# Spectrum in pairs, a shorter way from the last pieces to the first token blocks, and the last gate at the activation, in a state-space and token-mixing kernel on one core

## The chip, the cores and the metric

The kernel runs on one core of a Trainium2 chip. The metric is the device time of one execution in microseconds (us), given as the median of several runs. The core has five engines with an instruction stream each: TensorE (PE; its weight loads stand as PEld), VectorE (DVE), ScalarE (ACT), GpSimd (POOL) and SyncE (SP), which here issues DMA transfers. Engines wait for each other by semaphores.

## The reference

The input x has 2048 tokens of 448 channels, all float32. A vector c gives six modulation vectors; the block applies a long convolution with a kernel made from a state-space model (through an FFT of length 4096), then a two-layer network across tokens:

```python
x = A_u
mod = (_silu(c) @ w_mod).reshape(c.shape[0], 6, 1, -1)
sa, ca, ga, sb, cb, gb = (mod[:, 0], mod[:, 1], ...)
h = _layernorm(x) * (1 + ca) + sa
x = x + ga * _A_ref(h, ...)      # y = irfft(rfft(h) * rfft(K)) + h * D_skip
h = _layernorm(x) * (1 + cb) + sb
x = x + gb * _B_ref(h, ...)
# _B_ref: h = layernorm(x); u = gelu(w1^T over tokens + b1), 1792 wide;
#         y = w2^T over those + b2, 2048 tokens
```

## The kernel before

The work runs in five stages.

**The kernel and the spectrum** (to about 348 us of the span). TensorE makes the convolution kernel from the state-space parameters and the spectrum of h. The spectrum lies in DRAM as `us_d`, split into two halves of the channels ("chunks", 224 channels each, `DC`).

**The pieces.** Each chunk has 16 pieces (`NP`) of two frequencies. Piece n asks for its part of the spectrum (`u`) and its table (`si`) in `pc_load`; ACT makes a copy with the two halves of the partitions exchanged (`pc_swap`, tile `sw`), POOL completes the table with three operations (`pc_tables`), TensorE makes the convolution kernel's spectrum (`pc_s2`, tile `kx`), DVE multiplies (`pc_mul`, tiles `z0`, `z1`), TensorE transforms a first step back (`pc_inv`, tile `vv`), and ACT copies the result to SBUF (tile `vt` of `pc_out`), from where it is written to `v_d` in DRAM. The first chunk's pieces 0 to 15 are spread over the stage before. The second chunk's, 16 to 31, are the loop near the end of the listing: at step k the load of piece n+3, `kx` and the products of piece n, the table and the exchanged copy of piece n+1, and the way back of piece n−1.

**The head of the network.** The 2048 tokens are 16 blocks r of 128. `ln_load` reads a block's rows back from `v_d` (again tiles called `vt`), `ln_y` makes the last transform step with the table `ft` into PSUM (`y`) and adds it to x, and `stats`, `ln_mod` and `ln_out` make the two layer norms in a row, whose result is kept as a high and a low part (`h3h`, `h3l`). Until the first blocks are ready `warm` issues multiplies whose result nothing reads.

**The first layer**, `mlp1`: 14 tiles of 128 hidden units, in two halves of seven accumulators `acc`, each over the 16 blocks, with three matmuls for each pair (high by high, high by low, low by high). `gelu` empties the seven accumulators through ACT into `u`, of which three buffers exist, and DVE splits it into `uh` and `ul`. Both parts of a half are made in that order, f = 0 to 6, and the next half begins in the same order.

**The second layer**: 16 token tiles, each 42 matmuls into `o`, then bias, gate and residual on DVE and the write to the output.

Three more things set the order. PE, ACT, DVE and POOL run in the order of the code. SP does so too where a `manual_schedule` of SP is open (from step k = 12 of the second chunk on); before that a scheduler places its transfers. SP's queue is in order: a transfer whose data isn't ready holds up those behind it, and each waits for the one eight before it. The weights come through `wst`: `load` asks for one, `ahead` (or `begin` and `rest`) splits one into `whi` on ACT and `wlo` on DVE.

Of the kernel before, what the change touches and what calls it, by code (L numbers as in the profile page):

```python
# [15 lines left out]
ALU = mybir.AluOpType  # L16
# [21 lines left out]
WAHEAD = 4  # L38


def dft_tables():
# [66 lines left out]
    order = lambda a: a.reshape(P, 32, 2, 2, 2, 16).swapaxes(3, 4)  # L108
# [11 lines left out]
    t["FT"] = ft.reshape(P, 64)  # L120

# [99 lines left out]
def tile_adaln_s4d_mixer(ctx, tc, i, out):  # L221
# [20 lines left out]
    with ExitStack() as es:  # L242
# [520 lines left out]
        pl, pz, pv, pk = {}, {}, {}, {}  # L763
# [4 lines left out]
        def pc_load(n):  # L768
            c, p = divmod(n, NP)
            u = fp.tile([P, 2, 2, DC], F32, tag="u", name="u", bufs=3)  # L770
            if c:
                nc.sync.dma_start(u[:, 0], us_d[c, :, 2 * p : 2 * p + 2])
# [3 lines left out]
            w = fp.tile([P, 3, 2, P], F32, tag="si", name="si", bufs=4)  # L776
# [4 lines left out]
            pl[n] = u, w  # L781
# [3 lines left out]
        def pc_swap(n):  # L785

            pw[n] = swp.tile([P, 2, DC], F32, tag="sw", name="sw")
            for h in range(2):
                S.copy(pw[n][64 * h : 64 * h + 64], pl[n][0][64 - 64 * h : 128 - 64 * h, 0])

        def pc_tables(n):


            like, unlike = pl[n][1][:, 1], pl[n][1][:, 2]
            G.tensor_copy(unlike[0:64], like[64:128])
            G.tensor_copy(unlike[64:128], like[64:128])
            G.tensor_scalar(like[64:128], like[0:64], -1.0, None, ALU.mult)

        def pc_s2(n):
            c, p = divmod(n, NP)  # L800
            k1 = yks[c][:, 2 * p : 2 * p + 2]
            pk[n] = (pxs if c else pms).tile([P, 2, DC], F32, tag="ms", name="kx")
            for j in range(2):
                T.matmul(pk[n][:, j], pl[n][1][:, 0, j], k1[:, j], start=True, stop=True)  # L804

        def pc_mul(n):
            c, p = divmod(n, NP)
            u = pl[n][0]
            pz[n] = []
            for cc in range(2):  # L810
                z = fp.tile([P, 2, DC], F32, tag=f"z{cc}", name=f"z{cc}")
                V.tensor_tensor(z, pk[n], pw.pop(n) if c and cc else u[:, cc], ALU.mult)  # L812
                pz[n].append(z)
            pk.pop(n)

        def pc_inv(n):
            pv[n] = pms.tile([P, 2, DC], F32, tag="ms", name="vv")
            w, z = pl.pop(n)[1], pz.pop(n)
# [4 lines left out]
        def pc_out(n, copy=S.copy):  # L823
            c, p = divmod(n, NP)
            vt = swp.tile([P, 2, DC], F32, tag="vt", name="vt", bufs=4) if c else fp.tile([P, 2, DC], F32, tag="vt", name="vt")
            copy(vt, pv.pop(n))
            rows = v_d[2 * p : 2 * p + 2, :, c * DC : (c + 1) * DC]
# [342 lines left out]
        swp = es.enter_context(tc.tile_pool(name="swp", bufs=2))  # L1170
        pc_swap(NP)
# [27 lines left out]
        for n in range(2):  # L1199
            wst.ahead(n + 1, nc.vector, False)  # L1200


    with ExitStack() as es:
# [9 lines left out]
        v_v = v_d.rearrange("k (ch g r) d -> r (k ch) g d", ch=4, g=2)  # L1213
# [12 lines left out]
        vts, hs, sa, sb = {}, {}, {}, {}  # L1226

        def ln_load(r):
            vts[r] = rot.tile([P, 2, D], F32, tag="vt", name="vt", bufs=4)
            nc.sync.dma_start(vts[r], v_v[r])  # L1230
# [6 lines left out]
        def stats(src, total, tag):  # L1237

            mean, ss, rs = (small(nm, tag) for nm in ("mean", "ss", "rs"))
            V.tensor_scalar(mean, total, -1.0 / D, None, ALU.mult)  # L1240
            sq = rot.tile([P, D], F32, tag="sq", name="sq")
            S.activation(sq, src, AF.Square, bias=mean, accum_out=ss)
            S.activation(rs, ss, AF.Sqrt, scale=1.0 / D, bias=eps_t)
            return mean, rs

        def ln_y(r):
            y = py.tile([P, D], F32, tag="y", name="y")
            vt = vts.pop(r)
            for g in range(2):
                nc.tensor.matmul(y[64 * g : 64 * g + 64], ft, vt[:, g], start=True, stop=True)  # L1250
# [33 lines left out]
        for r in range(4):  # L1284
            ln_load(r)
            if r == 1:
                x_pair(2)
# [8 lines left out]
        for t in range(-3, 16):  # L1296
            if t < 0:
                warm((9, 1, 2)[t + 3])
# [33 lines left out]
        def gelu(acc, fh):  # L1332
            for f in range(7):
                k = 7 * fh + f
                u = ru.tile([P, D], F32, tag="u", name="u")
                S.activation(u, acc[f], AF.Gelu_apprx_tanh, bias=b1[:, k : k + 1])
                V.tensor_copy(uh[fh][:, f], u)
                V.tensor_tensor(ul[fh][:, f], u, uh[fh][:, f].bitcast(F32), ALU.subtract)
# [14 lines left out]
        for t in range(16):  # L1353
# [14 lines left out]
            V.scalar_tensor_tensor(y, o, b2[:, t : t + 1], mod[5], ALU.add, ALU.mult)  # L1368
            V.tensor_tensor(y, y, xt, ALU.add)
# [28 lines left out]
```

## Time and profile before

| | |
|---|---|
| median of three runs | 698.44 us (696.92 to 700.45) |
| the profiled execution | 699.5 us |
| its span | 697.7 us, mean granted clock 0.988 |
| TensorE busy | 646.5 us |
| second chunk, first `kx` to last `vv` | 354.81 to 393.53 us |
| first matmul of `mlp1` | 408.49 us |
| first activation of `gelu`, first half | 488.08 us |
| last matmul's first follower on DVE | 693.28 us |

The rows that follow are from one profiled execution. A timeline row has the start, the duration, the engine, the line of the code, the operation, out<-in, partitions and elements, how many instructions it stands for, and in brackets the idle time before it with what ended it. TensorE's records overlap, since matmuls are pipelined: the distance from one start to the next is the cost of one. "SPq" is SP issuing a transfer, "DMA" the transfer itself.

### The profile page before, as it was taken

The page shows a single profiled execution, that of the slowest core. Times are in us where ns is not written, and L with a number is a line of the kernel's source. Part 1 is how long each engine was busy: PE and PEld are TensorE (multiplying, and loading weights), DVE is VectorE, ACT ScalarE, POOL GpSimd, SP SyncE. Part 2 cuts the span into 40 slices and gives each one's busy share as a digit, 9 for nine tenths or more (in the row PEclk, how much of TensorE's full clock was granted, in tenths as well). Part 3 has the DMA queues.
Part 4 walks back from the last instruction along what each step waited for, and adds up shares of the span by engine and source line. Part 5 has one row for each costly group of instructions (what it writes and reads, how often), then busy time and mean ns, then how long its engine had stood idle before and what let it go on. Part 6 is the DMA issues. An engine that isn't in the chain of part 4 may idle for free.

```text
span 697.7 us, 18532 instructions
## 1 busy us (share of the span) xinstructions
PE 646.5 (93%) x7314; PEld 486.1 (70%) x7314; DVE 424.1 (61%) x811; ACT 448.5 (64%) x841; POOL 274.7 (39%) x364
## 2 busy tenths in 40 slices
PE   0868999999988899999999989999999999999997
PEld 0444454455545676676789747778999999999996
DVE  7877889787575584857744368777622354444431
ACT  5787698899879899999766568877422332222220
POOL 6694669588588767777546200000000000000000
PEclk9998999999999999999999999999999999999999
DMA  7595647588785486554579899974683445555640
GB/s 183 178 194 143 214 163 241 212 234 268 213 266 165 126 170 170 145 157 120 142 235 301 257 278 244 236 177 135 174 247 108 146 132 159 159 158 165 169 129 28
DMA packets 101894, 128.04 MB, mean 184 GB/s; under 512 B 13547, under 2 KB 85231, under 8 KB 101807
## 3 DMA queue, kind: packets, MB, share of 16 engines
q1 hardware_dynamic: 100606, 123.31, 63.0%
q0 software_dynamic: 1200, 3.54, 2.4%
q8 instruction: 58, 0.95, 0.6%
q14 instruction: 30, 0.24, 0.1%
HBM read 91.46 MB, written 34.87 MB: 181 GB/s over the span
## 4 chain that ended last, share of the span: by engine, by line
PE 68%; ACT 10%; DMA 8%; DVE 6%; issue 4%; POOL 3%; SPq 1%; DVEq 0%; ACTq 0%; POOLq 0%
PE xe L621 7%; PE acc L1222 7%; PE o L1365 6%; PE o L1364 6%; PE o L1366 6%; PE acc L1223 6%; PE acc L1224 6%; PE kg L711 6%; DMA si<-in_SK_dram 3%; PE xg L621 3%; PE pu L542 2%; PE pu L574 2%; PE vv L820 2%; PE kx L804 2%; PE vv L821 2%
## 5 line engine op out<-in xcount | busy, mean ns | idle before, releaser
L206 ACT CAST whi<-w 128x896 fp32r<-128x896 f32 x64 | 59.8, 938 | 134.9 <-PE o L1365 84.6
L215 DVE TENSOR_TENSOR wlo<-w,whi 128x896 fp32r<-128x896 f32 x64 | 68.1, 1088 | 43.1 <-ACT whi L206 36.8
L684 POOL TENSOR_TENSOR G<-mag,gs 128x512 f32<-128x512 f32 x56 | 71.9, 1283 | 50.9 <-ACT gs L680 47.1
L1222 PE MATMUL acc<-h3h,whi 128*128 128x448 f32 x224 | 82.7, 369 | 0.8 <-ACT h3h L1273 0.8
L1223 PE MATMUL acc<-h3l,whi 128*128 128x448 f32 x224 | 81.5, 364 | 0.7 <-DVE h3l L1280 0.5
L1365 PE MATMUL o<-ul,whi 128*128 128x448 f32 x224 | 81.3, 363 | 0.0
L1364 PE MATMUL o<-uh,whi 128*128 128x448 f32 x224 | 81.2, 362 | 0.0
L1224 PE MATMUL acc<-h3h,wlo 128*128 128x448 f32 x224 | 80.7, 360 | 0.0
L1366 PE MATMUL o<-uh,wlo 128*128 128x448 f32 x224 | 80.6, 360 | 0.0
L711 PEld LDWEIGHTS kg<-E,G 128*32 128x32 f32 x3584 | 56.6, 114 | 32.3 <-issue 22.2
L711 PE MATMUL kg<-E,G 128*32 128x64 f32 x3584 | 66.4, 228 | 6.7 <-issue 6.1
L685 POOL TENSOR_TENSOR G<-mag,gs 128x512 f32<-128x512 f32 x56 | 71.8, 1282 | 0.0
L621 PE MATMUL xg<-tab,lph 64*128 64x512 f32 x112 | 62.3, 556 | 5.1 <-ACT gs L680 2.4
L621 PE MATMUL xe<-tab,lph 64*128 64x512 f32 x112 | 62.2, 555 | 1.1 <-ACT gs L681 0.9
L686 DVE TENSOR_TENSOR E<-m,xe 128x512 f32<-128x512 f32 x53 | 36.4, 687 | 41.3 <-ACT xe L679 24.3
L1368 DVE SCALAR_TENSOR_TENSOR y<-o,b,mod 128x448 f32<-128x448 f32 x16 | 10.9, 684 | 80.2 <-PE o L1366 80.2
L665 POOL TENSOR_TENSOR m<-mag,w 128x512 f32<-128x512 f32 x53 | 56.0, 1056 | 4.3 <-DMA u<-us_d 0.2
L1222 PEld LDWEIGHTS acc<-h3h,whi 128*128 128x128 f32 x224 | 42.0, 188 | 13.9 <-ACT h L1278 5.6
L812 DVE TENSOR_TENSOR z<-kx,u 128x448 f32<-128x448 f32 x48 | 28.4, 620 | 27.7 <-PE kx L804 27.7
L1223 PEld LDWEIGHTS acc<-h3l,whi 128*128 128x128 f32 x224 | 42.1, 188 | 3.3 <-DVE h3l L1280 0.8
L1364 PEld LDWEIGHTS o<-uh,whi 128*128 128x128 f32 x224 | 42.0, 188 | 3.4
L621 PE MATMUL xe<-tab,lex 64*128 64x512 f32 x56 | 28.9, 531 | 16.6 <-DMA lex<-wm 15.8
(233 smaller groups left out, 1512.1 us busy)
## 6 DMA issues: line engine op xcount, KB each, us to landing
w<-in_B_w_dram SPq DMA_DIRECT2D x64, 224.0 KB
w<-in_B_w_dram SPq DMA_DIRECT2D x32, 448.0 KB
u<-us_d SPq DMA_DIRECT2D x48, 224.0 KB
yu_d<-yt SPq DMA_DIRECT2D x16, 448.0 KB
yi<-yu_d SPq DMA_DIRECT2D x32, 224.0 KB
us_d<-uo SPq DMA_DIRECT2D x16, 448.0 KB
v_d<-vt SPq DMA_DIRECT2D x32, 224.0 KB
vt<-v_d SPq DMA_DIRECT2D x16, 448.0 KB
```

Source lines behind the costliest of these rows:

```text
L206: self.nc.scalar.copy(hi, w)
L215: eng.tensor_tensor(lo, w, hi.bitcast(F32), ALU.subtract)
L621: T.matmul(out[k], lhs[r], rhs[r], start=start, stop=stop)
L684: G.tensor_tensor(Gt[:, 1], mg_, v32(sg), ALU.mult)
L685: G.tensor_tensor(Gt[:, 0], mg_, v32(cg_), ALU.mult)
L711: T.matmul(kg[32 * q : 32 * q + 32, m], Gt[:, c, d], E[:, c, d], start=h == 0 and c == 0 and m == 0, stop=h == 1 and c == 1, skip_group_ch ...
L1222: nc.tensor.matmul(acc[f], hi[:, fs], h3h[:, r], start=r == 0, stop=False)
L1223: nc.tensor.matmul(acc[f], hi[:, fs], h3l[:, r], start=False, stop=False)
L1224: nc.tensor.matmul(acc[f], lo[:, fs], h3h[:, r], start=False, stop=r == 15)
L1364: nc.tensor.matmul(o, hi[:, ks], uh[kh][:, k], start=kh == 0 and k == 0, stop=False)
L1365: nc.tensor.matmul(o, hi[:, ks], ul[kh][:, k], start=False, stop=False)
L1366: nc.tensor.matmul(o, lo[:, ks], uh[kh][:, k], start=False, stop=kh == 1 and k == 6)
```

## The change

1. The second chunk's spectrum is read for two pieces in one transfer (128 rows of 896 numbers instead of twice 448), four pieces ahead. Its tables have two more buffers, in another pool, and are asked for five pieces ahead instead of three. SP's transfers run in the order of the code from the end of step k = 0.
2. The rows of `v_d` are laid out in another order, by which a block's read has one run of both halves (`g`) for a row. Blocks 0 and 1 are read in two parts: the first chunk's columns at k = 2 and 4, the second chunk's columns of the first 26 rows at k = 14 (`v_half`). The last three pieces (`LAST`) go to these two blocks out of SBUF, by six matmuls for a block with the new table `fl`, which POOL clears with three memsets of 32 x 1536 and a transfer of 192 KB fills.
3. The first weight and the first pair of x are asked for at k = 11, the second weight at k = 12, and the first weight is split before the last copy of a piece.
4. `stats` takes the square with the sum as bias and D as scale, so that ACT doesn't wait for DVE's mean.
5. `warm` has 1, 1 and 3 multiplies instead of 9, 1 and 2.
6. The last gate `mod[5]` is multiplied to `u` behind the activation, not at the output: 14 more DVE operations of 128 x 448. In the second half the cast to `uh` goes to ACT. At the output `mod[5] * b2 + xt` is made before the matmuls end, and one addition stays behind them.

The diff, cut:

```diff
-            u = fp.tile([P, 2, 2, DC], F32, tag="u", name="u", bufs=3)
             if c:
-                nc.sync.dma_start(u[:, 0], us_d[c, :, 2 * p : 2 * p + 2])
+                nc.sync.dma_start(u.rearrange("p n k d -> p (n k d)"), us_d[c, :, 2 * p : 2 * p + 4].rearrange("p k d -> p (k d)"))
+                pu[n], pu[n + 1] = u[:, 0:1], u[:, 1:2]
...
+        def pc_w(n, pool=None):
+            c, p = divmod(n, NP)
+            w = (pool or fp).tile([P, 3, 2, P], F32, tag="si", name="si", bufs=2 if pool else 4)
...
+            if n >= 2 * NP - LAST:
+                vlast.append(vt)
...
+        v_v = v_d.rearrange("k (r ch g) d -> r k ch g d", ch=4, g=2)
+        end = 2 * (NP - LAST)
+        fl = swp.tile([P, 2, 2 * LAST, P], F32, name="fl", bufs=1)
...
+        def v_half(r, d0, k):
+            for g in range(2):
+                nc.sync.dma_start(vts[r][0 : 4 * k, g, d0 : d0 + DC], v_v[r, 0:k, :, g, d0 : d0 + DC])
...
             if k < NP:
-                if n + 3 < 2 * NP:
-                    pc_load(n + 3)
+                if k % 2 == 0 and n + 4 < 2 * NP:
+                    pc_u(n + 4)
+                for m in range(n + 5 if k else n + 3, n + 6):
+                    if m < 2 * NP:
+                        pc_w(m, swp if (m - NP) % 6 in (4, 5) else None)
...
-            if k == NP - 4:
+            if k == 0:
                 last = ExitStack()
                 last.enter_context(tc.manual_schedule(engines={ENG.SP}))
 
-            if k == NP - 3:
+            if k == 1:
+                for q in range(1, 4):
+                    G.memset(fl[32 * q : 32 * q + 32], 0.0)
+                nc.sync.dma_start(fl[0:32].rearrange("p r q m -> p (r q m)"), i["FL"])
+            if k in (2, 4):
+                r = k // 2 - 1
+                v_tile(r)
+                v_half(r, 0, 2 * NP)
+            if k == NP - 5:
                 wst.load()
                 x_pair(0)
-
-        wst.load()
+            if k == NP - 4:
+                wst.load()
+            if k == NP - 2:
+                for r in range(2):
+                    v_half(r, DC, end)
+            if k == NP - 1:
+                wst.ahead(1, nc.vector, False)
...
+            S.activation(sq, src, AF.Square, bias=total, scale=-float(D), accum_out=ss)
+            S.activation(rs, ss, AF.Sqrt, scale=1.0 / D**3, bias=eps_t)
             V.tensor_scalar(mean, total, -1.0 / D, None, ALU.mult)
...
+                nc.tensor.matmul(out[:, 0:DC], ft, vt[:, g, 0:DC], start=True, stop=True)
+                nc.tensor.matmul(out[:, DC:], ft[0:n], vt[0:n, g, DC:], start=True, stop=False, skip_group_check=True)
+            for q in range(2 * LAST) if r < 2 else ():
+                p, k = divmod(q, 2)
+                nc.tensor.matmul(y[:, DC:], fl[:, r, q], vlast[p][:, k], start=False, stop=q == 2 * LAST - 1, skip_group_check=True)
...
-                warm((9, 1, 2)[t + 3])
+                warm((1, 1, 3)[t + 3])
...
+                S.activation(us[f], acc[f], AF.Gelu_apprx_tanh, bias=b1[:, k : k + 1])
+                V.tensor_tensor(us[f], us[f], mod[5], ALU.mult)
+                if fh == 0:
+                    split(f, V.tensor_copy)
+                elif f:
+                    split(f - 1, S.copy)
...
-            V.scalar_tensor_tensor(y, o, b2[:, t : t + 1], mod[5], ALU.add, ALU.mult)
-            V.tensor_tensor(y, y, xt, ALU.add)
+            V.scalar_tensor_tensor(xt, mod[5], b2[:, t : t + 1], xt, ALU.mult, ALU.add)
+            V.tensor_tensor(y, o, xt, ALU.add)
```

On SP, at the start of the second chunk, the transfers stand in this order before (the numbers tell tiles apart: si_6041 is the table of piece 16, si_6089 of 17, si_6109 of 18, si_6205 of 19; u_6039 is the spectrum of 16, u_6087 of 17, u_6107 of 18):

```order
L778 DMA si_6041<-in_SJ_dram 128x768
L828 DMA v_d_63<-vt_6036 128x2x224
L772 DMA u_6039<-us_d_62 128x448
L780 DMA si_6089<-in_SK_dram 128x512
L828 DMA v_d_63<-vt_6099 128x2x224
L772 DMA u_6087<-us_d_62 128x448
L780 DMA si_6109<-in_SK_dram 128x512
L828 DMA v_d_63<-vt_6119 128x2x224
L772 DMA u_6107<-us_d_62 128x448
L780 DMA si_6205<-in_SK_dram 128x512
```

And so now (u_6039 is the pair 16 and 17, u_6105 the pair 18 and 19, u_6202 the pair 20 and 21; si_6206 and si_6208 are the tables of 20 and 21 in the new buffers, si_6087 of 17, si_6107 of 18, si_6204 of 19):

```order
L789 DMA si_6041<-in_SJ_dram 128x768
L846 DMA v_d_63<-vt_6036 128x2x224
L778 DMA u_6039<-us_d_62 128x896
L791 DMA si_6206<-in_SK_dram 128x512
L791 DMA si_6087<-in_SK_dram 128x512
L846 DMA v_d_63<-vt_6097 128x2x224
L791 DMA si_6208<-in_SK_dram 128x512
L778 DMA u_6105<-us_d_62 128x896
L791 DMA si_6107<-in_SK_dram 128x512
L846 DMA v_d_63<-vt_6117 128x2x224
L778 DMA u_6202<-us_d_62 128x896
L791 DMA si_6204<-in_SK_dram 128x512
```

The tables of pieces 20 and 21 have moved ahead of those of 17 and 18, and between two writes of `v_d` there now stands twice the spectrum.

On PE, from the end of the second chunk to the first block of `mlp1`, before (`vv` is the last piece, `acc<-mod` a warm-up multiply, `y<-vt,ft` a token block, `acc<-h3h,whi` the first of `mlp1`):

```order
L821 MATMUL vv<-z_6574,si 128x224
L1294 MATMUL acc<-mod_68 128x448 x9
L1250 MATMUL y<-vt,ft 64x448 x2
L1294 MATMUL acc<-mod_68 128x448
L1250 MATMUL y<-vt,ft 64x448 x2
L1294 MATMUL acc<-mod_68 128x448 x2
L1250 MATMUL y<-vt,ft 64x448 x2
L1222 MATMUL acc<-h3h,whi 128x448
```

And now, to the second block:

```order
L837 MATMUL vv<-z_6576,si 128x224
L1350 MATMUL acc<-mod_68 128x448
L1303 MATMUL y<-vt,ft 64x224
L1304 MATMUL y<-vt,ft 64x224
L1303 MATMUL y<-vt,ft 64x224
L1304 MATMUL y<-vt,ft 64x224
L1307 MATMUL y<-vt,fl 128x224 x6
L1350 MATMUL acc<-mod_68 128x448
L1303 MATMUL y<-vt,ft 64x224
L1304 MATMUL y<-vt,ft 64x224
L1303 MATMUL y<-vt,ft 64x224
L1304 MATMUL y<-vt,ft 64x224
```

Eight of the nine multiplies ahead of block 0 are gone; the matmuls of the first two blocks are half as wide and twice as many, and six with `fl` follow them.

On DVE, in the first `gelu`, before (one f is a cast and a subtraction):

```order
L1337 CAST uh_6625<-u 128x448
L1338 TENSOR_TENSOR ul_6626<-u,uh_6625 128x448
L1337 CAST uh_6625<-u 128x448
L1338 TENSOR_TENSOR ul_6626<-u,uh_6625 128x448
L1337 CAST uh_6625<-u 128x448
L1338 TENSOR_TENSOR ul_6626<-u,uh_6625 128x448
```

And now:

```order
L1399 TENSOR_TENSOR u<-u,mod_70 128x448
L1392 CAST uh_6624<-u 128x448
L1393 TENSOR_TENSOR ul_6625<-u,uh_6624 128x448
L1399 TENSOR_TENSOR u<-u,mod_70 128x448
L1392 CAST uh_6624<-u 128x448
L1393 TENSOR_TENSOR ul_6625<-u,uh_6624 128x448
```

The multiplication by the gate stands ahead of each cast.

More of the change, by code (lines that the diff above doesn't have):

```diff
@@ L38 @@
 WAHEAD = 4
+LAST = 3
 def dft_tables():
@@ L1198, in tile_adaln_s4d_mixer @@
         V.memset(eps_t, EPS)
-        for n in range(2):
-            wst.ahead(n + 1, nc.vector, False)
+        wst.ahead(2, nc.vector, False)
     with ExitStack() as es:
@@ L1248, in ln_y @@
             vt = vts.pop(r)
+            n = 4 * end
             for g in range(2):
[L1250 removed]
+                out = y[64 * g : 64 * g + 64]
+                if r > 1:
+                    nc.tensor.matmul(out, ft, vt[:, g], start=True, stop=True)
+                    continue
+                nc.tensor.matmul(out[:, 0:DC], ft, vt[:, g, 0:DC], start=True, stop=True)
[3 more added lines that the diff above has]
+                nc.tensor.matmul(y[:, DC:], fl[:, r, q], vlast[p][:, k], start=False, stop=q == 2 * LAST - 1, skip_group_check=True)
             total = small("sum", "a")
@@ L1283, in tile_adaln_s4d_mixer @@
         first.enter_context(tc.manual_schedule(engines={ENG.SP}))
[L1284 to L1287, printed above, removed]
+        ln_load(2)
+        x_pair(2)
+        ln_load(3)
         wst.load()
```

56 lines of the change are left out of this document (35 added, 21 removed).

## The prediction

> **What bounds the kernel now.** I read the page first (span, engines, clock, chain), then the windows of ten microseconds from 340 on, since the first instructions on the compute engines that the change alters stand there, and then the timelines of PE, ACT, DVE and SP around each altered place.
>
> ```profile
> span 697.7 us, 18532 instructions
> PE 646.5 (93%) x7314; PEld 486.1 (70%) x7314; DVE 424.1 (61%) x811; ACT 448.5 (64%) x841; POOL 274.7 (39%) x364
> ...
> PEclk9998999999999999999999999999999999999999
> ...
> PE 68%; ACT 10%; DMA 8%; DVE 6%; issue 4%; POOL 3%; SPq 1%; DVEq 0%; ACTq 0%; POOLq 0%
> ```
>
> TensorE is busy for 93% of the span and holds 68% of the chain that ended last, at a clock that stays near full. The change takes no work from TensorE worth naming, so what it can win is TensorE's waits: all its idle time together is 697.7 − 646.5 = 51 us, most of it before 340, where the order of the work stays as it is. The stretch of the second chunk and the head behind it look like this (columns: window, length, then busy us of PE, PEld, DVE, ACT, POOL with counts, granted clock, DMA share, GB/s):
>
> ```profile
> 340.00:350.00 10.00, 9.16 (x219) 7.63 (x212) 6.07 (x10) 5.59 (x12) 3.40 (x4) 1.00 0.58 165
> 350.00:360.00 10.00, 9.38 (x105) 8.34 (x105) 3.91 (x7) 6.39 (x12) 4.92 (x9) 1.00 0.71 204
> 360.00:370.00 10.00, 10.00 (x54) 9.86 (x53) 5.44 (x10) 6.29 (x12) 4.90 (x9) 1.00 0.93 275
> 370.00:380.00 10.00, 9.51 (x51) 9.30 (x50) 4.62 (x8) 7.56 (x14) 6.89 (x13) 1.00 0.98 311
> 380.00:390.00 10.00, 9.80 (x52) 9.22 (x51) 4.62 (x8) 7.20 (x14) 6.58 (x14) 1.00 0.93 295
> ```
>
> From 360 to 390 the DMA engines are 93 to 98% busy at 275 to 311 GB/s, and TensorE is still 95 to 100% busy: the two limits lie close together here. The two windows before have room (165 and 204 GB/s).
>
> **Part 1: pairs of pieces and loads asked for earlier.**
>
> ```profile
> 354.81 1.68 PE L804 MATMUL kx<-yk,si 128*128 128x224 f32 x8
> ...
> 357.46 0.65 PE L821 MATMUL vv<-z,si 128*128 128x224 f32 x2 [0.37 <-DVE z L812]
> ...
> 358.70 0.92 PE L804 MATMUL kx<-yk,si 128*128 128x224 f32 x4
> ...
> 360.97 0.92 PE L804 MATMUL kx<-yk,si 128*128 128x224 f32 x4
> ...
> 369.67 0.54 PE L821 MATMUL vv<-z,si 128*128 128x224 f32 x2
> 370.70 1.02 PE L804 MATMUL kx<-yk,si 128*128 128x224 f32 x4 [0.49 <-DMA si<-in_SK_dram]
> ...
> 388.74 0.54 PE L821 MATMUL vv<-z,si 128*128 128x224 f32 x2
> 389.48 1.02 PE L804 MATMUL kx<-yk,si 128*128 128x224 f32 x4 [0.20 <-DMA si<-in_SK_dram]
> ...
> 392.99 0.54 PE L821 MATMUL vv<-z,si 128*128 128x224 f32 x2
> ```
>
> A piece takes 360.97 − 358.70 = 2.27 us of TensorE, so 16 pieces need 36.3 us; the stretch lasts from 354.81 to 392.99 + 0.54 = 393.53, which is 38.7. That point, the end of the last vv, is called T below. Two matmuls of a vv follow each other at 0.38 (0.54 is the two records overlapped), so without a wait the kx at 370.70 would start at 369.67 + 0.38 = 370.05 and that at 389.48 at 389.12: 0.65 and 0.36 are lost to late si tables. With 0.05 at a third place these waits are 1.06; the rest (0.37 at 357.46 and what goes with it) waits for the first piece's spectrum copies on ACT and stays.
>
> Does asking earlier help where the DMA engines are full? The bytes of this stretch are 3.67 MB spectrum (16 × 128 × 448 × 4), 3.93 MB tables (15 × 128 × 512 × 4), 2.75 MB v written up to piece 27 (12 × 224 KB), and, new, 0.66 MB: the table fl and the first-half columns of two token blocks. That is 11.0 MB.
>
> ```profile
> 346.07 0.33 SPq L772 DMA_DIRECT2D u<-us_d  x1
> ...
> 384.81 4.63 DMA si<-in_SK_dram
> ```
>
> Issues begin at 346.07; at the 300 to 311 GB/s that the full windows reach, 11.0 MB take 35 to 37 us, so the last table lands about 382, against 384.81 + 4.63 = 389.4 now and a need at 388. The early requests fill the windows with 165 and 204 GB/s. I take the whole 1.06: **−1.1** (0 if the queue is the limit at every moment; −1.5 with part of the 0.87 that the start loses). What is late next is TensorE itself.
>
> The three memsets of fl go on POOL between two pieces' tables.
>
> ```profile
> L315 POOL MEMSET lex<- 32x256 f32 x4 | 1.2, 340 | 0.0
> ...
> L490 POOL MEMSET sums<- 1x128 f32 x4 | 0.9, 225 | 0.2
> ...
> 355.14 0.84 POOL L797 TENSOR_SCALAR si<-si 64x256 f32<-64x256 f32 x1
> ```
>
> From 225 ns at 128 elements to 340 at 256 it is 0.9 ns an element: 1536 elements take 1.5 us (2.0 in plain proportion to the 340), three of them 4.5 (6.1). The tables of piece 18 end at 355.98 now; memsets and then the 1.8 of piece 19's own tables bring those to 362.3 (363.9), and its vv needs them at 360.97 + 0.76 + 2.27 = 364.0. Costed at nothing. The cover is thin: piece 18's si is now queued behind piece 20's and behind a pair of spectra, and each us by which that makes it late beyond 1.7 is a us of wait at vv(19); I keep +1.9 for two us late with the dear memsets, so that part 1 reaches from −1.5 to +0.8.
>
> **Part 2: the end of the chunk and the first two token blocks.**
>
> ```profile
> 393.61 0.53 ACT L826 COPY vt<-vv 128x448 f32<-128x448 f32 x1 [1.03 <-PE vv L821]
> ...
> 394.17 3.22 DMA v_d<-vt
> ...
> 397.47 1.22 SPq L1230 DMA_DIRECT2D vt<-v_d  x2
> ...
> 394.20 7.03 PE L1294 MATMUL acc<-mod 128*128 128x448 f32 x18 [0.67 <-ACT vt L826]
> 401.37 0.97 PE L1250 MATMUL y<-vt,ft 128*64 128x448 f32 x4
> ...
> 406.00 0.61 DVE L1253 SCALAR_TENSOR_TENSOR xt<-xt,y 128x448 f32<-128x448 f32 x1
> ...
> 406.11 0.67 ACT L1242 ACTIVATE sq<-h,mean 128x448 f32<-128x448 f32 x1 [1.73 <-DVE mean L1240]
> ...
> 415.72 0.62 DVE L1280 TENSOR_TENSOR h3l<-h,h3h 128x448 fp32r<-128x448 f32 x1
> ...
> 416.39 0.48 PE L1223 MATMUL acc<-h3l,whi 128*128 128x448 f32 x1 [0.54 <-DVE h3l L1280]
> ```
>
> Now the last copy (393.61) is written to DRAM in 3.22 us, SP issues the read at 397.47, and y(0) starts at 401.37 = T+7.8; nine warm-up multiplies of 7.03/9 = 0.78 fill the gap. From h3l(1), which ends at 416.34 = T+22.8, the MLP runs without a wait. After the change y(0) needs from DRAM only rows up to piece 28. The chain is: last copy as now; one warm-up from T+0.67, to T+1.45; y(0) with the same columns of ft (0.9) and six fl matmuls of 128x224 at 0.38, in all 3.2, to T+4.7; a warm-up, to T+5.45; y(1), to T+8.6; its sum on DVE at T+8.7 where it starts at 406.00 = T+12.5 now. From there to the end of h3l(1) the trace has 10.3 us, less some 0.5 because the squares no longer wait for the mean (row 406.11; four statistics, about 0.15 of mean each): T+18.5. **−4.3** (−3 to −5). TensorE, which has block 0's products and two more y in between, comes to block 1 at about T+18.1, so it is late next by little.
>
> The cover is the transfer of piece 28. Its copy lies three pieces (6.8 us) before the last, so its write starts at about T−5.9 and lands at T−2.7 by 3.22, or T−1.3 by the 4.63 of the table above. Four reads of 93 KB are issued behind it, each at most the 0.61 of SP that a read takes in the row at 397.47, and land after another 3.22 at T+1.1 to T+2.9 (the last of them); the matmul that reads them is due at about T+1.9. Block 0's two come first, at about T+0.5 to T+1.9 by the first price, so no wait; with both transfers at 4.63 and the issues in a row it is some 2 us. The Trainium skill, "DMA: Bandwidth & Descriptors", section "Anatomy of one DMA — SWDGE (gpsimd) path", gives such a transfer about 2.0 us and its bytes at 436 GB/s, and says that most of the fixed part is the receipt of the last byte. As an estimate from that page a 93 KB read takes 2.2 us, a microsecond below the 3.22 of the row here, and the sum would be the same −4.3 with a margin; SP's queue isn't that path, so the row decides.
>
> What SP queues behind the four reads are the last three v writes and the weights; the writes of pieces 29 to 31 are then needed only by block 2, which has until T+10.
>
> **Part 3: the gate at the activation.**
>
> ```profile
> 488.08 2.49 ACT L1336 ACTIVATE u<-acc,b 128x448 f32<-128x448 f32 x4 [2.27 <-PE acc L1224]
> 490.88 0.64 ACT L1336 ACTIVATE u<-acc,b 128x448 f32<-128x448 f32 x1 [0.32 <-DVE ul L1338]
> ...
> 488.75 0.39 DVE L1337 CAST uh<-u 128x448 fp32r<-128x448 f32 x1 [2.42 <-ACT u L1336]
> 489.18 0.63 DVE L1338 TENSOR_TENSOR ul<-u,uh 128x448 fp32r<-128x448 f32 x1
> ...
> 495.08 0.36 PE L1222 MATMUL acc<-h3h,whi 128*128 128x448 f32 x1
> ```
>
> A u has three buffers: the fifth activation waits for a subtraction three back (row 490.88). DVE now spends 0.43 on the cast and 0.54 on the subtraction; with a multiply of the form of the subtraction ahead, whose result the cast needs (0.66), it is 1.62 for one f. The subtraction of f=3 then ends at 488.75 + 4 × 1.62 + 0.1 = 495.3, the seventh activation runs to 496.1, and TensorE, which overwrites that accumulator first at 495.08, waits **+1.0** (0.4 to 1.2). In the second half the cast goes to ACT; multiply and subtraction are about 1.2 for one f there, and TensorE first writes to its seventh accumulator's successor in mlp2, which began on the other outputs: nothing.
>
> **Part 4: the tail.**
>
> ```profile
> 693.28 0.68 DVE L1368 SCALAR_TENSOR_TENSOR y<-o,b,mod 128x448 f32<-128x448 f32 x1 [7.05 <-PE o L1366]
> 694.00 0.63 DVE L1369 TENSOR_TENSOR y<-y,x 128x448 f32<-128x448 f32 x1
> ```
>
> Only one of the two DVE operations stays behind the last matmul: **−0.7** (694.00 − 693.28). The other runs beside the matmuls, where DVE waited 7.05.
>
> **Sum.** −1.1 − 4.3 + 1.0 − 0.7 = −5.1. The profiled execution took 699.5 with 1.8 around its span; that gives 694.4. The median of the three runs is 698.44, 1.1 below it, so by the median **693.3**. The terms' ends give −1.5 − 5 + 0.4 − 0.7 = −6.8 and 0.8 − 3 + 1.2 − 0.7 = −1.7, so 691.6 to 696.7.
>
> **Rivals.** (a) The second chunk is bound by bytes anyway. For it: 93 to 98% DMA share over 30 us, and 0.66 MB of new bytes (2.1 us at 311 GB/s). Against: the empty windows ahead. Then part 1 gives 0, or with a part of those bytes on the path +1: 694.4 to 695.4. (b) The reads for the first two blocks come late, so that the change doesn't take the DRAM path off y(0) as it says: the 2 us worked out above, 695.3. For it: four issues and two transfers in a row while the queue still moves weights.
>
> (c) Slower: the clock. Twelve warm-up multiplies become five, and if TensorE's clock is granted by its recent work, a late y(0) costs twice. The Trainium skill, "TensorE: Matmul & The Clock Gate", Part 1, says that the clock falls to half after an idle window of about 3.4 us. Against it: all windows above show 1.00 with waits up to 1 us, and the forecast's longest wait is below 2. At half clock from y(0) to the first products, the 10.3 us of that stretch would be 10.3 longer at most; taking y(0) to y(2) and block 0's start, 6 us more than before at h3l(1) (T+28.8): −1.1 + 6.0 + 1.0 − 0.7 = +5.2, so 703.6. It decides only when y(0) waits for several us more than in (b). No row here shows such a drop, though the fourth slice of the PEclk line has an 8.
>
> **How the numbers follow.** The forecast has 0.68, (a) 0.13, (b) 0.12, (c) 0.05, and 0.02 is left for what I don't see. About 0.5% (3.5 us) is what a measurement of this kernel can tell from no change: faster means below 694.9, slower above 701.9. The forecast lies below 694.9 in most of its cases, (a) and (b) in a part of theirs: faster 0.73, same 0.20, slower 0.07. The range of 8 in 10 takes the forecast's ends, (a) and (b), and a little on both sides for the medians' spread (696.92 to 700.45): 690.9 to 697.0.
>
> **What would show it.** In the changed kernel: kx of pieces 23 and 31 without a DMA behind them, the vv's end 1 us earlier; y(0) starting at T+1.5 and followed by fl matmuls with no wait for vt; the granted clock still 1.00 from 390 to 420; block 1's first h3l product at T+18 to T+19; a wait of 1 us of TensorE for an activation at the seventh accumulator of the second half; one DVE operation behind the last matmul. A y(0) that waits for a DMA past T+3, a clock below 0.9 there, or a wait of TensorE for POOL's tables of piece 19 would make it wrong.

## The result and the profile after

The changed kernel takes 696.84 us (median of 20 runs, 694.30 to 699.62) against 700.11 for the kernel before in the same sessions: a ratio of 0.9952, 95% interval 0.9929 to 0.9974. That is 3.4 us less (1.8 to 5.0); the forecast was 5.1. It went the way it was said to, at about two thirds of the size. Against the 698.44 that the forecast started from, it is only 1.6 us less.

The profiled execution must be read with care. Its span is 692.6 us, 5.1 below that of before, which looks like the forecast to the tenth. But DVE's first product of piece 16, ahead of which the compute engines have the same order in both kernels, stands at 355.76 before and 352.43 after. On DVE's timeline, before:

```profile
355.76 0.62 DVE L812 TENSOR_TENSOR z<-kx,u 128x448 f32<-128x448 f32 x1 [2.69 <-PE kx L804]
```

And after, the page's first line and then DVE's timeline:

```profile
span 692.6 us, 18551 instructions
```

```profile
352.43 0.62 DVE L828 TENSOR_TENSOR z<-kx,u 128x448 f32<-128x448 f32 x1 [2.69 <-PE kx L820]
```

So 3.3 of the 5.1 us arose where nothing was changed. The windows of that stage show one source (the third number from the end of a row is the granted clock). Before:

```profile
220.00:230.00 10.00, 9.53 (x213) 6.42 (x213) 2.36 (x4) 8.58 (x18) 8.18 (x16) 0.83 0.94 230
230.00:240.00 10.00, 8.13 (x105) 5.64 (x104) 5.70 (x9) 9.91 (x19) 7.36 (x8) 0.87 0.45 122
```

After:

```profile
220.00:230.00 10.00, 9.68 (x189) 6.08 (x178) 1.29 (x2) 9.77 (x20) 9.45 (x16) 1.00 1.05 259
230.00:240.00 10.00, 8.11 (x157) 5.37 (x155) 8.41 (x14) 8.07 (x16) 7.99 (x7) 0.83 0.29 85
```

The clock is 0.50 for 3.4 us from 220.36 and from 237.43 before (the second runs past 240), and from 233.17 after: one such stretch less. By the clock of the profile before, DVE is 1.25 us earlier in the profile after already at 202, 2.8 earlier behind the stretch that is missing, and gains the last 0.5 at 341. Over the 13 profiles of this study that product starts anywhere from 351.60 to 356.64, and in e1, which has before's loads, at 354.39. One profile's span against another's is therefore no measure of this change; the lengths of its own stages are:

| stage, us | before's code | changed code | forecast |
|---|---|---|---|
| second chunk: first product on DVE to last copy on ACT | 37.85, 38.22 | 36.53 to 36.57 in 4 of 5 profiles, 38.09 in one | −1.1 |
| head: last copy to first activation | 94.46, 95.89, 95.25 | 93.30, 92.54; 97.82 with the clock halved | −4.3 |
| first activation to first matmul of layer two | 70.60, 70.60 | 71.75 in each | +1.0 |
| last matmul's first follower on DVE to the span's end | 4.44, 4.46 | 4.01, 4.02, 4.02 | −0.7 |

("Before's code" are the profiles of before and of the experiments e1 and f4, each for the stages that it leaves alone; "changed code" those of the changed kernel, its repeat g1, e4, f1 and g2, likewise.) The middles of the two columns, without the halved clock, give −1.5 − 2.3 + 1.15 − 0.4 = −3.1 us, which agrees with the −3.4 of the runs. Only the head is far off its forecast.

The chunk after, by windows: the stretch from 340 to 360 now moves 260 and 238 GB/s instead of 165 and 204, and from 360 to 380 there is no wait of TensorE left:

```profile
340.00:350.00 10.00, 8.90 (x185) 7.34 (x175) 4.70 (x8) 3.11 (x7) 2.25 (x5) 1.00 0.84 260
350.00:360.00 10.00, 9.57 (x49) 8.92 (x50) 4.66 (x8) 7.99 (x15) 8.28 (x11) 1.00 0.79 238
360.00:370.00 10.00, 10.00 (x55) 10.00 (x54) 4.63 (x9) 7.38 (x14) 8.97 (x18) 1.00 1.05 358
370.00:380.00 10.00, 10.00 (x54) 10.00 (x53) 5.54 (x10) 7.55 (x14) 8.84 (x17) 1.00 1.01 351
```

The head after, on TensorE's timeline. The last vv ends at 388.87, which is T here:

```profile
389.54 1.02 PE L1350 MATMUL acc<-mod 128*128 128x448 f32 x2 [0.67 <-ACT vt L842]
...
391.54 0.40 PE L1304 MATMUL y<-vt,ft 104*64 104x224 f32 x1 [0.46 <-DMA vt<-v_d]
...
392.52 0.59 PE L1304 MATMUL y<-vt,ft 104*64 104x224 f32 x2 [0.38 <-DMA vt<-v_d]
393.05 2.54 PE L1307 MATMUL y<-vt,fl 128*128 128x224 f32 x12
395.42 0.92 PE L1350 MATMUL acc<-mod 128*128 128x448 f32 x2
...
402.85 0.48 PE L1270 MATMUL acc<-h3h,whi 128*128 128x448 f32 x1
...
409.47 0.97 PE L1301 MATMUL y<-vt,ft 128*64 128x448 f32 x4 [1.04 <-DMA vt<-v_d]
...
410.68 0.36 PE L1271 MATMUL acc<-h3l,whi 128*128 128x448 f32 x1
```

Block 0's ft matmuls take from 390.4 to 393.05, 2.65 us instead of 0.9, because the second halves of its rows come late, and block 4's rows make TensorE wait for another 1.04. The last row is block 1's first h3l product, for which the forecast worked out its 4.3 us: it starts at T+21.8, where it was T+22.9 before and was to be T+18.5. SP's timeline shows the queue:

```profile
382.48 1.25 SPq L192 DMA_DIRECT2D w<-in_B_w_dram  x2
383.82 2.23 SPq L846 DMA_DIRECT2D v_d<-vt  x2
388.80 3.51 SPq L1199 DMA_DIRECT2D vt<-v_d  x4
```

And the chain of waits from 380 to 412 the transfers themselves:

```profile
383.82 4.93 DMA v_d<-vt
...
400.72 8.61 DMA vt<-v_d
```

Piece 28 is copied by 383.4 and its write waits for SP, which is issuing the second weight until 383.73. It then takes 4.93 us and lands at T−0.1, where the forecast had T−2.7. The four reads take 3.51 us to issue, 0.88 each. The read of block 4 goes out at T+11.9 behind x and weights and takes 8.61.

The gate and the tail, on the timelines of ACT, TensorE and DVE:

```profile
489.60 0.63 ACT L1398 ACTIVATE u<-acc,b 128x448 f32<-128x448 f32 x1 [0.98 <-DVE ul L1393]
...
489.18 0.36 PE L1272 MATMUL acc<-h3h,wlo 128*128 128x448 f32 x1
490.28 0.47 PE L1270 MATMUL acc<-h3h,whi 128*128 128x448 f32 x1 [0.74 <-ACT u L1398]
490.59 0.36 PE L1271 MATMUL acc<-h3l,whi 128*128 128x448 f32 x1
...
688.60 0.62 DVE L1436 TENSOR_TENSOR y<-o,x 128x448 f32<-128x448 f32 x1 [7.18 <-PE o L1433]
```

The seventh activation waits for a subtraction and TensorE for the activation, as forecast. Matmuls follow each other at 0.20 there; the two distances from 489.18 to 490.59 are 1.10 and 0.31, which is 1.0 us more. One operation stands behind the last matmul.

### The profile page after: what moved, and what is told of

Read it like the earlier page. It is cut to its first block, busy times and chain, and to the rows that moved or that the text cites. A ratio compares the mean times of both kernels' runs of the same rounds, so it can differ in the third digit from the quotient of the medians.

```text
span 692.6 us, 18551 instructions
## 1 busy us (share of the span) xinstructions
PE 643.8 (93%) x7332; PEld 487.5 (70%) x7332; DVE 428.5 (62%) x818; ACT 451.4 (65%) x848; POOL 279.0 (40%) x367
## 4 chain that ended last, share of the span: by engine, by line
PE 72%; ACT 9%; DVE 5%; DMA 4%; issue 4%; POOL 2%; SPq 2%; DVEq 0%; ACTq 0%; POOLq 0%
PE xe L627 8%; PE o L1432 7%; PE o L1431 6%; PE o L1433 6%; PE acc L1270 6%; PE acc L1271 6%; PE acc L1272 6%; PE kg L717 6%; PE xg L627 3%; PE vv L836 3%; PE kx L820 3%; PE vv L837 3%; PE pu L548 3%; PE pu L580 2%; PE kg L639 2%
## 5 line engine op out<-in xcount | busy, mean ns | idle before, releaser
L717 PE MATMUL kg<-E,G 128*32 128x64 f32 x3584 | 64.8, 225 | 4.8 <-issue 4.0
L1436 DVE TENSOR_TENSOR y<-o,x 128x448 f32<-128x448 f32 x16 | 10.0, 627 | 78.8 <-PE o L1433 78.8
L1272 PEld LDWEIGHTS acc<-h3h,wlo 128*128 128x128 f32 x224 | 41.9, 187 | 3.1
```

Of the source, the lines that this page charges most:

```text
L717: T.matmul(kg[32 * q : 32 * q + 32, m], Gt[:, c, d], E[:, c, d], start=h == 0 and c == 0 and m == 0, stop=h == 1 and c == 1, skip_group_ch ...
L1272: nc.tensor.matmul(acc[f], lo[:, fs], h3h[:, r], start=False, stop=r == 15)
```

## The experiments

T is the end of the last vv in each kernel; the stages are those of the table. Every kernel was run beside the kernel before, and ratios are against it.

**e1, the gate alone.** Before, with `gelu` and the output as in the change:

```diff
+                V.tensor_tensor(us[f], us[f], mod[5], ALU.mult)
...
-            V.scalar_tensor_tensor(y, o, b2[:, t : t + 1], mod[5], ALU.add, ALU.mult)
-            V.tensor_tensor(y, y, xt, ALU.add)
+            V.scalar_tensor_tensor(xt, mod[5], b2[:, t : t + 1], xt, ALU.mult, ALU.add)
+            V.tensor_tensor(y, o, xt, ALU.add)
```

> The kernel before with the gate at the activation alone (the edit of gelu and of the output). In the profile of the changed kernel TensorE waits 0.74 us for the seventh activation of the first half, and the distance from the last matmul's follower on DVE to the span's end fell from 4.4 to 4.0 us. If these two are all that the gate does, this kernel's span from its first block of the second half's matmuls to the end is +0.74 - 0.4 = +0.3 us against before, and its time the same within what can be measured. If the 14 more DVE operations and the casts on ACT also hold up weight splitting (the rival), waits of TensorE for whi or wlo show in either half and the stretch behind 488 is longer by more than 1 us. This run also gives a second profile of the stage ahead of the second chunk, which is that of before word for word: the changed kernel reached the chunk 3.3 us earlier than before, at the first vv wait (349.19 before, 345.86 after). If that was chance of one execution, this run's value lies anywhere between or beyond; if the changed kernel is really faster there, this run has 349.

Measured: ratio 1.0014 (0.9992 to 1.0036). From the first activation to the second layer 71.75 us, 1.15 more than before; last matmul's first follower on DVE to the end 3.95. So the gate costs 1.15 − 0.5 = 0.7 us; the second layer between these two stages is as long as before (134.6 us from its first matmul to the follower in all three profiles). Of the 1.15, 1.0 is lost at the seventh accumulator, by the distances from start to start, and 0.13 at the sixth. The first product on DVE stands at 354.39, between the two profiles.

**e2, the second weight late.**

```diff
-            if k == NP - 4:
-                wst.load()
...
+        wst.load()
         last.close()
```

> The changed kernel with the second weight asked for behind the chunk's last v write instead of at step 12. Theory A (the gain of the head was lost because piece 28's write was issued at T-5.05 behind that weight and took 4.93 us beside it, so that the four reads were issued from T-0.07 on): without the weight the write goes out at about T-6 and takes 3.2 to 3.6, the reads go out from about T-2.5, y(0) has at most 0.3 us of wait, and T to the last matmul of y(5), 25.9 us in the changed kernel, becomes 24.0 to 24.5. Rival B (the reads themselves are slow: four issues of 0.78 to 0.95 with the last two v writes behind them): y(0) waits as before, and the stretch stays at 25.5 to 26. A second cost may come in: the second weight's split is later, and TensorE would wait for it at block 1, by up to 1 us.

Measured: ratio 0.9959 (0.9935 to 0.9982), head 91.41 us, 1.9 less than the changed kernel's 93.30. T is 392.86 here. The reads go out at T−1.8, and neither ft matmul of block 0 waits:

```profile
387.40 0.37 SPq L846 DMA_DIRECT2D v_d<-vt  x1
...
391.08 3.67 SPq L1199 DMA_DIRECT2D vt<-v_d  x4
...
394.48 0.60 PE L1302 MATMUL y<-vt,ft 128*64 128x224 f32 x4
394.91 0.59 PE L1303 MATMUL y<-vt,ft 104*64 104x224 f32 x4
```

That is theory A. Piece 28's write goes out at T−5.5 instead of T−5.05 and SP is released some 3.6 us later, not 4.93: of the 1.7 us by which the reads are earlier, 0.4 is SP's time for the weight and 1.3 the shorter transfer. The four issues still take 3.67 us, so rival B alone explains nothing. T to y(5) is 24.0 us, as expected, and TensorE does not wait for the second weight; y(4) still waits 0.69 for its rows. Against the repeat of the changed kernel (g1, 92.54) the gain is 1.1, not 1.9. Against the 95.2 that before's code has on average the head gains 3.8 now, close to the forecast 4.3; against the one profile that the forecast was made from it is 3.0. The median of the runs (696.5) does not tell this kernel from the changed one; the stage does.

**e3, the loads of the second chunk as before, within the changed kernel.**

```diff
-                for m in range(n + 5 if k else n + 3, n + 6):
-                    if m < 2 * NP:
-                        pc_w(m, swp if (m - NP) % 6 in (4, 5) else None)
+                if n + 3 < 2 * NP:
+                    pc_load(n + 3)
```

> The changed kernel with the second chunk's loads as before: one piece of spectrum at a time, asked for three pieces ahead, no further table buffers. If the early requests are what removed the DMA waits, the waits of kx for si come back: about 1.1 us more between the first kx and the last vv, with the transfers between 360 and 390 spread at about 300 GB/s instead of 350 in the first part. If the chunk is the same (within 0.3 us), it was SP's fixed order or the memory layout that removed them. The rows of fl and the reads of the first two blocks, 0.66 MB more, could make it 2 us.

Measured: ratio 1.0062 (1.0029 to 1.0095), chunk 44.12 us: 7.6 more, not 1.1 to 2. On TensorE's timeline, the last kx:

```profile
373.42 1.02 PE L819 MATMUL kx<-yk,si 128*128 128x224 f32 x4 [0.88 <-DMA si<-in_SK_dram]
...
393.19 1.86 PE L819 MATMUL kx<-yk,si 128*128 128x224 f32 x4 [3.53 <-DMA si<-in_SK_dram]
```

And in the window behind it:

```profile
393.00:396.00 3.00, 2.81 (x8) 2.55 (x9) 0.91 (x2) 0.78 (x2) 1.64 (x3) 0.50 0.67 201
```

Here the last table is asked for at 387.17, behind the first weight and the first pair of x (both from 383.91 on), and takes 5.99 us; in the changed kernel the last table goes out at 376.08. The last kx waits 3.53 us. Then the clock is 0.50 and the kx takes 1.86 instead of 1.02. The stall also delays T, so the reads for blocks 0 and 1 go out at T−3.1; block 0 doesn't wait, although the second weight is early here, and the head is 91.99.

**f4, part 1 alone, on the kernel before** (the same edit in the other direction, and SP in the order of the code from step 0).

> The kernel before with part 1 alone: spectrum in pairs, further table buffers, tables five pieces ahead, SP in the order of the code from step 0. From the first product of piece 16 on DVE to the last copy on ACT it was 37.85 us before (38.22 with the gate alone), 36.53 in the changed kernel, and 44.12 in the changed kernel with the loads as before. By the prediction's part 1 this kernel has 36.5, too, with no wait of kx for si. If the early requests only make room for the 0.66 MB that the change adds and for its earlier weights, and do nothing by themselves, it has 37.8. The head is that of before: last copy to y(0) 7.8 to 9.1 us.

Measured: chunk 36.53 us, ratio 0.9989 (0.9966 to 1.0012), y(0) 8.55 behind the last copy. So part 1 gains its 1.3 to 1.7 alone, as forecast, and e3 adds that the rest of the change could not do without it. SP's fixed order is not what does it, since e3 has that order too; reading in pairs and asking earlier were not tried apart.

**e4, no warm-ups.**

```diff
-                warm((1, 1, 3)[t + 3])
+                warm((0, 0, 0)[t + 3])
```

> The changed kernel without its five warm-up multiplies. By theory A the three ahead of y(2) stand on TensorE's path in part: the first block's h3h is written at 401.55 and TensorE reaches mlp1 at 402.85, so T to the end of y(5) becomes 0.5 to 1.3 us shorter, and the granted clock stays 1.00 up to 420. By the clock theory (TensorE idles for 3 us or more in the head and the clock drops) the granted clock between 390 and 420 falls below 1.00 and the stretch gets longer by 2 to 6 us. If DVE and ACT set the pace of the head, the stretch is the same within 0.3 us.

Measured: ratio 0.9984 (0.9965 to 1.0003), head 93.35 us, as in the changed kernel. `mlp1` began 1.5 us earlier and gave it back at y(4):

```profile
391.03 0.40 PE L1304 MATMUL y<-vt,ft 104*64 104x224 f32 x1 [1.96 <-DMA vt<-v_d]
...
409.18 0.97 PE L1301 MATMUL y<-vt,ft 128*64 128x448 f32 x4 [2.14 <-DMA vt<-v_d]
```

And the window with the second of these waits:

```profile
400.00:410.00 10.00, 7.53 (x33) 4.28 (x33) 7.63 (x24) 7.79 (x19) 0.00 (x0) 1.00 1.04 265
```

In this profile the clock stayed at 1.00 with waits of 1.96 and 2.14, and T to y(5) is what it was in the changed kernel (25.9 us), as the third expectation has it; but the rows of block 4 set the pace, not DVE and ACT.

**f1, the cast on ACT in the first half too.**

```diff
-                if fh == 0:
-                    split(f, V.tensor_copy)
-                elif f:
+                if f:
                     split(f - 1, S.copy)
```

> The changed kernel with the first half's cast to uh on ACT, as it has it in the second half. From the first activation to the first matmul of the second layer it is 70.60 us before and 71.75 in the changed kernel (1.15 more, 0.74 of it the wait at the seventh accumulator). With DVE at 0.54 + 0.54 for an f and ACT at about 1.2, the seventh activation ends some 7.9 us behind the first one's start, where TensorE needs it at 7.0 behind: if ACT's 1.2 is the pace a wait of 0 to 0.3 is left and the stretch is 70.6 to 70.9. If the 1.15 come from elsewhere (weight splits on DVE behind the longer row), the stretch stays above 71.3.

Measured: ratio 0.9943 (0.9916 to 0.9971); first activation to second layer 70.60 us: the whole 1.15 is back. But this profile's span is 697.8, for two stalls where nothing was edited. On TensorE's timeline, and in one of the windows behind the second stall:

```profile
362.67 0.65 PE L836 MATMUL vv<-z,si 128*128 128x224 f32 x2 [1.30 <-POOL si L813]
...
413.15 1.76 PE L1301 MATMUL y<-vt,ft 128*64 128x448 f32 x4 [2.85 <-DMA vt<-v_d]
```

```profile
414.00:416.00 2.00, 2.00 (x7) 1.08 (x4) 1.02 (x6) 1.17 (x2) 0.00 (x0) 0.50 1.05 212
```

vv(19) waits for POOL's tables behind the memsets: POOL began piece 18's tables 1.9 us later here than in the changed kernel's profile, counted from the first product on DVE, and what held them up the profile doesn't name. And y(4) waits 2.85 us for its rows, near the end of which the clock falls to 0.50. The halved stretch lasts 6.8 us, and the head is 97.82.

**f2 and f3, block 4's rows earlier**, on e2; f3 with f1's cast as well.

```diff
         ln_load(3)
+        ln_load(4)
+        x_pair(4)
         wst.load()
```

> The second weight behind the last v write, and block 4's rows asked for ahead of the fourth pair of x and the third weight. In the changed kernel y(4) waited 1.04 us for its rows, whose transfer was 8.61 us from its issue behind 0.9 MB of x and weight, and 0.69 with the second weight late. If that order is the cause, y(4) has no wait, and from the last copy to the first activation it is 90.4 to 91.0 us (93.30 in the changed kernel, 91.41 with the second weight late). If it only moves the wait to the x pair or the third weight, which are now behind, it is 91.4 or more, with a wait of DVE for xt or of TensorE for whi at block 2.

> The last two together: the second weight late, block 4's rows early, the first half's cast on ACT. If the stages add up, it is 2.5 us less from the last copy to the first activation and 0.9 less from there to the second layer than the changed kernel: 3.4 us below it, a ratio of about 0.991 to 0.993 against before. If the stages don't add (the wait goes elsewhere), it is the same as the changed kernel within 1 us.

Measured: f2 0.9927 (0.9898 to 0.9956), f3 0.9922 (0.9896 to 0.9948). y(4) no longer waits, but the heads are 92.20 and 92.28, no better than e2's 91.41: TensorE waits 0.70 (0.38 in f3) for a later h3l on DVE. The second half of that expectation held: the wait moved. f3's ratio lies where it was expected, 0.003 or 2.1 us below the changed kernel's, but the intervals overlap, and its two stages (92.28 and 70.60) add up to 2.2 us less, not to 3.4.

**g1, the changed kernel again, and g2, block 4's rows earlier with the second weight early.**

> The changed kernel once more, unaltered, for a second profile and more times. The changed kernel with the cast on ACT had, in its profile, two stalls that the changed kernel's own profile doesn't have: 1.30 us at vv(19) for POOL's tables, and 2.85 at y(4) followed by a granted clock of 0.50 for 6.8 us, 4.5 us in the head. Neither place is touched by that cast. If such stalls belong to the changed kernel and come and go with the run, this profile has one of the three heads seen (93.3 without, up to 97.8 with), a chunk of 36.5 or 38.1, and the twelve further times spread over 5 us again (694.3 to 699.6 in twenty). If they come from the cast, chunk and head are 36.5 and 93.3 within 0.3.

> The changed kernel with block 4's rows asked for ahead of the fourth pair of x and the third weight, and the second weight where the change puts it. If y(4)'s wait for its rows is what makes the head vary, y(4) has no wait, the granted clock stays 1.00 from 390 to 430, y(0) still waits about 1 us (its cause is left), and the head is 92 to 93 us. With the second weight late this order gave 92.2, and block 2 then waited 0.7 for DVE. If the two waits are independent, the median is 1 to 2 us below the changed kernel's; if the wait only moves, it is the same.

Measured: g1 0.9960 (0.9931 to 0.9988), head 92.54 us with no wait at y(4) at all, chunk 36.53. So y(4)'s wait comes and goes: 1.04, 0 and 2.85 in three profiles with the same order. g2 0.9956 (0.9933 to 0.9978), and its head, 94.77, was longer, by a stall at y(0), on TensorE's timeline and in a window behind it:

```profile
392.08 0.40 PE L1304 MATMUL y<-vt,ft 104*64 104x224 f32 x1 [1.82 <-DMA vt<-v_d]
...
392.99 4.22 PE L1307 MATMUL y<-vt,fl 128*128 128x224 f32 x12
```

```profile
394.00:396.00 2.00, 2.00 (x7) 1.82 (x6) 0.00 (x0) 0.00 (x0) 0.00 (x0) 0.50 0.41 139
```

The reads were late, TensorE waited, and the twelve fl matmuls behind it took 4.22 us instead of 2.54, at a clock of 0.50 in part. y(4) has no wait here, but the median, 696.45, is the changed kernel's.

**g3, fl cleared and loaded at step 6**, on f3.

```diff
-            if k == 1:
+            if k == 6:
                 for q in range(1, 4):
```

> Second weight late, block 4's rows early, cast on ACT, and the memsets and the transfer of fl at step 6 instead of step 1. POOL's three memsets took 4.22 us between the tables of pieces 18 and 19, and in one of nine profiles vv(19) waited 1.30 us for them. At step 6 POOL is several pieces ahead, so no vv waits for POOL: chunk 36.5 us always, and the time is that of the same kernel with the memsets at step 1 (694.1) or up to 0.5 below. If POOL isn't ahead by then, vv(24) waits by up to 2 us and the chunk is 38.

Measured: 0.9929 (0.9908 to 0.9951), chunk 36.52, head 91.25, no stall from 360 to 560. As f1's stall is one in a few profiles, one profile without it doesn't show that the move cures it.

## Why the prediction was right or wrong

**Right.** Part 1: both waits for si are gone, chunk −1.3 to −1.7 for −1.1; f4 shows that part 1 alone does it. Part 3: +1.15 for +1.0, with the third-back subtraction as its cause; e1 has it alone and f1 takes it away. POOL's memsets, on POOL's timeline of the changed kernel, took 4.22 us for 4.5:

```profile
354.19 4.22 POOL L1228 MEMSET fl<- 32x1536 f32 x3
```

They were hidden in eight of the nine profiles that have them at step 1, and the thin cover that was named did fail once, at vv(19), by 1.30.

**Wrong by size: the head, −2.3 instead of −4.3.** The step that failed is "the cover is the transfer of piece 28": its write was to land at T−2.7 to T−1.3 and the reads to cost no wait. I priced the write from its ACT copy at 3.22 us and took SP as free, although the change itself (its point 3) puts the second weight, two issues of 1.25 us together and 448 KB, between that copy and its write. The write landed at T−0.1, 2.6 us later than T−2.7: 1.7 because the transfer took 4.93, 0.4 because SP was busy with the weight, and 0.4 because the copy itself lies nearer to the last one than I counted (the last two copies stand 1.55 apart, not 2.27, since no kx is between them). The reads were issued in 0.88 each for my 0.61, and block 0 lost 1.75 us. y(0) waited for a DMA until T+3.65, past the T+3 that the prediction named as a sign against it. e2 moves the weight alone: both ft waits of block 0 are gone (of the three further profiles with this weight late f3 keeps 0.33, f2 and g3 nothing), and the head gets 1.1 to 1.9 us back. This was rival (b), priced at 2 and given 0.12: its price was about right and its chance too low.

A second step failed in the same place: "block 2, which has until T+10". I let SP's later reads cost nothing. Block 4's rows are issued at T+11.9 behind x and weights and make TensorE wait from nothing to 2.85 us. TensorE is through with the work ahead of y(4) at T+19.6 now, at T+20.9 before: part of the gain ahead of it turned into this wait. These two steps account for most of the sign that did not come: block 1's first h3l product at T+18 to T+19 was at T+21.8, and in e2, where only the second wait is left, at T+19.9.

**Rival (c) happened, in some runs.** I gave the clock 0.05 and asked for a y(0) that waits several us more than in (b). In two of the five profiles that have the change's loads and its early second weight (the changed kernel, g1, e4, f1, g2) the clock halved in the head, after waits of 1.82 (g2, at the very y(0)) and 2.85 us (f1); in the others waits of 0.77, 1.04, 1.96 and 2.14 left it at 1.00. As an estimate from half the busy time at half clock it cost 1.7 us in g2 and 3.1 in f1, not the 10 of a whole stretch, since it lasted 3.4 and 6.8 us. In none of the four profiles with the second weight late did it happen in the head. The rule of the Trainium skill ("TensorE: Matmul & The Clock Gate", Part 1) that I set against the traces bears on this kernel after all, though shorter waits than its 3.4 us window sufficed here.

**The tail**, −0.4 to −0.5 for −0.7. DVE's second operation is gone from the end, but the stretch from the remaining one's end to the span's end is 3.4 us where it was 3.1. Why it got longer was not tried. In the three profiles with the cast on ACT in both halves (f1, f3, g3) the whole stage is 3.76 to 3.80 instead of 4.0, so it does not hang on the output's code alone.

The forecast 693.3 was made against a median of three runs, 698.44; over 90 further runs the kernel before has 699.4, so about 1 us of the distance to 696.84 lies in that reference.

## What to carry to other kernels

Before a transfer is counted as hidden, list what its queue issues between the moment its data is ready and its own issue, including what the same change puts there; a weight that is asked for early was in the way of the one write that mattered. Work that only keeps TensorE busy also covers for late transfers: where it is taken out, price the late case with the clock halved for 3.4 us or more, because in this case it happened in part of the runs. (That the taken multiplies would have prevented it is argued; no run has the change with the old number of them.) And where runs differ by several us, compare the lengths of the stages that a change touches, not spans: here 3.3 of the 5.1 us between two profiles were chance.

## What the runs showed of the hardware

A granted clock of 0.50 came in stretches of 3.4 us or twice that, at or near waits of TensorE of 1.82, 2.85 and 3.53 us, and not at others of 1.96 and 2.14. The length of a wait alone does not decide it; its place does as well. Inside one execution all these stretches begin on one grid of 3.413 us, to within 0.05 us: in f1 at 218.03, 235.10 and 412.59, which lie 5 and 52 steps apart, in e3 at 225.38, 235.62 and 392.63, 3 and 46 steps apart. All 13 profiles show this, each with its own offset. Windows cut on that grid, first f1's and the one behind it, then g2's and e4's:

```profile
409.18:412.59 3.41, 1.12 (x6) 0.71 (x4) 3.05 (x8) 2.60 (x7) 0.00 (x0) 1.00 1.05 224
412.59:416.01 3.42, 2.86 (x7) 1.41 (x8) 1.53 (x8) 2.17 (x6) 0.00 (x0) 0.50 1.04 229
```

```profile
389.96:393.38 3.42, 1.59 (x10) 0.86 (x9) 1.15 (x2) 1.03 (x2) 0.00 (x0) 1.00 0.43 96
```

```profile
407.45:410.86 3.41, 1.68 (x8) 0.96 (x9) 2.46 (x8) 2.69 (x7) 0.00 (x0) 1.00 1.06 255
```

From 350 to 560 us, over all 13 profiles, the three windows in which TensorE is busy least (0.44 us in e3, 1.12 in f1, 1.59 in g2) are just those that half clock follows; the next, e4's 1.68, is followed by 1.00. e4's two waits each straddle an edge of its grid (390.38 and 407.45), so that no window holds more than 1.73 us of one. This measure does not carry to the stage ahead, where the matmuls are smaller: there half clock followed windows with up to 3.06 us busy.

At 0.50 a matmul of 448 columns followed the next at 0.375 us instead of 0.20. Over the 20 runs of the changed kernel the mean clock goes from 0.982 to 0.995 and the time falls with it (correlation −0.67; −0.72 over 90 runs of before), so about half of the spread between runs of this kernel (the squares, 0.45 and 0.52) goes with the clock.
